# The order of three groups of transfers on SyncE's queue, around a full DMA stretch of a linear-attention and squared-ReLU kernel

## Chip, cores and metric

The kernel runs on one core of a Trainium2 chip. The metric is the device time in microseconds; the median of three runs is given. One further execution was recorded by the profiler.

## The reference

```python
# q, k, v: (8, 8, 576, 64) float32; g_norm: (64,)
kv  = np.einsum('bhsd,bhse->bhde', k, v)
out = np.einsum('bhsd,bhde->bhse', q, kv)
rms = np.sqrt(np.mean(out * out, axis=-1, keepdims=True) + 1e-06)
x   = (out / rms * g_norm)          # then (B,H,S,D) -> (B*S, H*D): 4608 x 512
# w_in: (512, 2048), w_out: (2048, 512), both float64
h = x @ w_in
g = np.maximum(h, 0.0) ** 2
result = g @ w_out                  # 4608 x 512, float32
```

## The kernel before, in words

The work is cut into nine strips of 512 tokens (`for s in range(N_STRIP)`, L1186). Each strip has an up projection with `w_in`, the squared ReLU, and a down projection with `w_out`. Both products are done as seven block products each in place of eight, so the weights are needed as blocks and as sums of blocks. The attention of the coming strips is written in slices between the steps of the projections (`attend`). The order of all instructions is written out by hand: each engine executes its own in the order in which the code issues them. All DMAs that matter here are issued by SyncE (SP) and go into one queue. In the built program each of SP's DMAs also waits, where nothing earlier implies it, for the DMA eight places before it.

The change lies in the first strip (`s == 0`). Its up projection takes 16 steps (`n_up`), its down projection 14 more: seven products in the order 1, 2, 5, 6, 7, 3, 4, two steps each. A step calls `down` (L863), which multiplies (L733), and after a product's second step adds its result into an output or keeps it (`combine`; o_sb at L895 and L897) and may fetch a coming block of `w_out` (`stream`, L828). The sixth product is product 3; its block is the w_blk loaded in the second product's second step, `i == n_up + 3`. The seventh is product 4. PSUM banks are shared: products 1, 6, 7 and 4 use bank A, 5 and 3 bank B, 2 bank C. Product 4 adds into bank A after VectorE has read product 7's result from it.

These parts stand around the change:

- `store_first(b)` (L327, DMA at L329) writes one of three blocks of `w_out`, which the conversion left in unused places of `w_in` in SBUF, to DRAM, in two DMAs of 512 KB. Block 2 is the one moved. These places are needed again: `sums_in` (L295 to L302, subtractions by the helper at L288) writes sums of `w_in` there, so its VectorE instructions wait until the store has read them.
- `load_next(names="kv")` (L131) loads keys and values of one pair of heads, two DMAs of 256 KB. It is called twice, for the third batch's first two pairs.
- `load_rest(2, nc.sync)` (L161) loads keys and values of the third batch's last 64 tokens, two DMAs of 128 KB in rows of 256 B. PE reads both in `key_value` (L431), in the second strip.
- `store_deep_sums` (L849) computes four sums of a `w_out` block on VectorE (tile w_t) and stores them to `w_deep` (L855, L861).

Of the kernel before, what the change touches and what calls it, by code (L numbers as in the profile page):

```python
# [20 lines left out]
def kernel(  # L21
# [135 lines left out]
    def load_rest(b, eng):  # L157
        h = b % 2
        half = slice(REST * h, REST * (h + 1))
        for t, src in ((k_rest[half], k), (v_rest[half], v)):  # L160
            eng.dma_start(out=t, in_=src[b, :, C * P : S].rearrange("h s d -> s h d"))  # L161

    def load_q_rest(b, eng, one=None):
        h = b % 2
        if h == 0 and not one:
            q_rest[b // 2] = rest_pool.tile([P, H, D], FP32, name="q_rest", tag="q_rest")
        src = q[b, :, C * P : S]
        if b < Q_ON_PE:
            eng.dma_start(out=q_rest[b // 2][REST * h : REST * (h + 1)], in_=src.rearrange("h s d -> s h d"))
            return  # L170
        t = squares(q_rest[b // 2])
        for a in range(4) if one is None else (one,):
            hq, f = divmod(a * SQ, D)
            for kq in range(2):
                eng.dma_start(
                    out=t[ts(a, SQ), 2 * h + kq], in_=src[hq::2, ts(kq, SQ), f : f + SQ].rearrange("p i f -> i p f")
                )
# [4 lines left out]
    def load_next(q_eng=nc.sync, names="kvq"):  # L182
        u = next(to_load, None)
        if u is not None:
            load(*u, q_eng, names)
# [6 lines left out]
    def due(queue):  # L192
        if queue and queue[0][0] <= clock[0]:
            _, f, a = queue.popleft()
            f(*a)
            return True
# [4 lines left out]
    def drip(rest=False):  # L201
        for d in (drips, rest_drips) if rest else (drips,):
            if d:
                f, a = d.popleft()
                return f(*a)
# [121 lines left out]
    def store_first(b):  # L327
        for e in range(2):
            nc.sync.dma_start(out=w_out[b, :, e], in_=w_first[b][:, :, ts(e, P)])  # L329

    def convert(n):
        while converted[0] < min(n, len(conversions)):
            fn, a = conversions[converted[0]]
            fn(a)
            converted[0] += 1
# [356 lines left out]
    def attend(n):  # L692
        while slice_at[0] < min(n, len(slices)):
            fn, a = slices[slice_at[0]]
            fn(*a)
            slice_at[0] += 1
# [60 lines left out]
    def sum_g1(s, g):  # L757
        dest = quarters(s, g)
        s1 = gq[s, 1, g] = sum_pool.tile([P, 2, TH], FP32, name="g_s1", tag="sum")
        nc.vector.tensor_tensor(out=s1, in0=dest[12], in1=dest[22], op=ALU.add)  # L760

    def sum_g3(s, g):
        dest = quarters(s, g)
        minus(nc.vector, dest[12], dest[11], dest[12])
# [165 lines left out]
    def leaf_sums(s, p):  # L930
        deque(leaf_steps(s, p), 0)
# [254 lines left out]
    for s in range(N_STRIP):  # L1186
        attend(ready[s])
        if s == DEEP_UP - 1:
            while queried:
                attend(slice_at[0] + 1)  # L1190
            psums.close()
            fpsum = ctx.enter_context(tc.tile_pool(name="fpsum", bufs=5, space=bass.MemoryType.PSUM, reuse_waits="tile"))
            apsum = ctx.enter_context(tc.tile_pool(name="apsum", bufs=1, space=bass.MemoryType.PSUM, reuse_waits="tile"))
        if s >= DEEP_UP:
            steps = [(0.5, up_slot, (s, slot)) for slot in range(55)]
        elif s == 0:
            steps = [(2, up_first, (g, fh, i)) for g in range(NG) for fh in range(2) for i in range(2)]
        else:
            steps = [(1, up, (s, g, p)) for g in range(NG) for p in ORDER]
        n_up = len(steps)  # L1200
        if s < DEEP:

            steps += [(2, down, (s, p, i)) for p in (ORDER if s else (1, 2, 5, 6, 7, 3, 4)) for i in range(2)]
        else:
            steps += [(2, down_deep, (s, k, i)) for k in range(7) for i in range(2)]
        goal, begun = ready.get(s + 1, len(slices)), slice_at[0]
        if s >= DEEP_UP:
            goal = max(goal, min(ready[DEEP_UP] + (len(slices) - ready[DEEP_UP]) * (s - 1) // (N_STRIP - DEEP_UP - 1), len(slices)))
        total, done = sum(w for w, _, _ in steps), 0
        for i, (w, fn, a) in enumerate(steps):  # L1210
            if s == 0 and i < n_up:

                if 4 <= i < 10:
                    convert(3 + i)
                if i == 0:
                    load_next()
                    load_rest(1, nc.sync)
                    load_next()
                if i == 1:
                    load_next()  # L1220
                if i == 2:
                    for b in range(2):
                        load_q_rest(b, nc.sync)
                if i == 14:
                    for b in range(2):
                        store_first(b)
            elif s == 0 and i == n_up:
                convert(len(conversions))
                conv.close()

                stream_pool = ctx.enter_context(tc.tile_pool(name="stream", bufs=4, reuse_waits="tile"))
                sum_pool = ctx.enter_context(tc.tile_pool(name="sum", bufs=8, reuse_waits="tile"))
            if s == 0 and n_up <= i < n_up + 2:
                for g in range(2 * (i - n_up), 2 * (i - n_up) + 2):
                    sum_g1(0, g)
            if s == 0 and n_up + 2 <= i < n_up + 4:
                for g in range(2 * (i - n_up) - 4, 2 * (i - n_up) - 2):
                    sum_g3(0, g)
            fn(*a)
            if s == 0 and i < 4:  # L1240

                convert(3 + i)
            done += w
            if s:
                clock[0] += 3.2 if i >= n_up else 2.2 if s == DEEP else 1.2
                soon = tiles_due and tiles_due[0][2][0] // NT == s + 1
                if i == n_up + 10:
                    while tiles_due and tiles_due[0][2][0] // NT == s + 1:
                        _, f, a = tiles_due.popleft()
                        f(*a)  # L1250
                elif not due(keys_due) and not (soon and due(tiles_due)):
                    least = 2.1 if s == DEEP else 4.5 if i < n_up else 3.3
                    quiet = n_up * 2 // 3 < i < n_up + 3 or s == DEEP and i > n_up + 5
                    if not quiet and clock[0] >= dripped[0] + least:
                        dripped[0] = clock[0]
                        drip(True)
                pace = 25 if s == DEEP else 36
                attend(begun + (goal - begun) * min(i + 1, pace) // pace)
                if s == DEEP and i == n_up - 3:
                    leaf_sums(s, 4)  # L1260
                if s == 1 and i in range(2, 23, 3):
                    deep_sums_in((1, 6, 5, 4, 0, 2, 3)[i // 3])
                if s == 1 and i in (21, 22, 23, 25):
                    stream()
                continue
            if i == n_up:
                stream(2)
            if i == n_up + 3:
                store_first(2)
            if i in (n_up + 8, n_up + 11):  # L1270
                load(2, (i - n_up) // 11, nc.sync, "q")
            if i == n_up + 12:
                load_q_rest(2, nc.sync)
            if i - n_up in (7, 8, 9, 12):
                sums_in((7, 8, 9, 12).index(i - n_up))
            if i == n_up + 11:
                sums_x(1)
            n = i + 1 - (n_up - 6)
            pairs, m = divmod(max(n - 2 * NP, 0), 3)
            attend(min(ready[0] + min(max(n, 0), 2 * NP) + (n >= 2 * NP) + 4 * pairs + (0, 2, 2)[m], goal))  # L1280
            if i == n_up + 6:
                stream()
            while deep_due and i not in (n_up + 1, n_up + 4):
                store_deep_sums(*deep_due.popleft())
            if i == n_up + 2:
                for _ in range(2):
                    load_next(names="kv")
                load_rest(2, nc.sync)
            if 11 <= i < n_up:

                convert((13, 13, 14, 15, 16)[i - 11])
# [30 lines left out]
```

## Time and profile before

| | us |
|---|---|
| median of three runs | 899.84 (899.05 to 900.23) |
| profiled execution, device time | 901.59 |
| span of its instructions | 899.4 |
| TensorE busy | 881.8 |
| VectorE busy | 734.8 |
| ScalarE busy | 315.3 |
| GpSimd busy | 306.6 |
| mean DMA rate over the span | 262 GB/s |
| mean granted TensorE clock | 0.998 |

Times in the profile count from the first instruction of the span. The profiled execution has its own time, 2.2 us more than its span and 1.75 us more than the median of the runs. In the rows, PE is TensorE's matmuls, PEld its weight loads, DVE VectorE, ACT ScalarE, POOL GpSimd and SPq the queue of SyncE, whose rows are DMA issues; "L733" is a line of the kernel; a bracket at the end of a row gives the idle time ahead of it and what ended it. A row of SPq shows how long the issue took. The trace gives the time from issue to landing separately.

### The profile page before, as it was taken

The page shows a single profiled execution, that of the slowest core. Times are in us where ns is not written, and L with a number is a line of the kernel's source. Part 1 is how long each engine was busy: PE and PEld are TensorE (multiplying, and loading weights), DVE is VectorE, ACT ScalarE, POOL GpSimd, SP SyncE. Part 2 cuts the span into 40 slices and gives each one's busy share as a digit, 9 for nine tenths or more (in the row PEclk, how much of TensorE's full clock was granted, in tenths as well). Part 3 has the DMA queues.
Part 4 walks back from the last instruction along what each step waited for, and adds up shares of the span by engine and source line. Part 5 has one row for each costly group of instructions (what it writes and reads, how often), then busy time and mean ns, then how long its engine had stood idle before and what let it go on. Part 6 is the DMA issues. An engine that isn't in the chain of part 4 may idle for free.

```text
span 899.4 us, 20683 instructions
## 1 busy us (share of the span) xinstructions
PE 881.8 (98%) x8296; PEld 824.0 (92%) x8296; DVE 734.8 (82%) x1256; ACT 315.3 (35%) x622; POOL 306.6 (34%) x315
## 2 busy tenths in 40 slices
PE   8999989999999999999999999999999999999998
PEld 7445878889999999999999999999999999999998
DVE  4999979779778986799688966986899779875886
ACT  4898241320026302540245013801271027102710
POOL 0000004900348223731474045704461446144700
PEclk9999999999999999999999999999999999999999
DMA  9998997999988798899886989799647865784385
GB/s 313 298 325 258 291 336 226 279 286 350 304 225 258 272 313 245 192 315 332 241 242 238 320 250 245 228 292 317 209 151 285 296 206 175 285 309 156 124 305 192
DMA packets 169231, 235.71 MB, mean 262 GB/s; under 512 B 79408, under 2 KB 134192, under 8 KB 160688
## 3 DMA queue, kind: packets, MB, share of 16 engines
q1 hardware_dynamic: 168976, 234.40, 81.1%
q8 instruction: 65, 1.06, 0.5%
q14 instruction: 30, 0.25, 0.1%
q10 hardware_dynamic: 160, 0.00, 0.0%
HBM read 197.66 MB, written 36.70 MB: 261 GB/s over the span
## 4 chain that ended last, share of the span: by engine, by line
PE 74%; DVE 10%; DMA 8%; ACT 4%; issue 2%; SPq 1%; DVEq 0%; ACTq 0%
PE ps_B L948 21%; PE ps_A L1136 16%; PE ps_A L948 16%; PE ps_B L1136 8%; PE ps_C L1136 4%; PE ps_A L733 3%; DMA v<-in_v_dram 2%; DMA w_blk<-w_deep 2%; PE kv_ps L431 2%; PE x_ps L467 2%; PE ps_B L733 1%; DVE gt L1148 1%; DMA w_out<-w_in 1%; ACT raw L253 1%; ACT w_c L250 1%
## 5 line engine op out<-in xcount | busy, mean ns | idle before, releaser
L948 PE MATMUL ps_B<-w_blk,g_s 128*128 128x128 f32 x1024 | 126.3, 276 | 0.0
L948 PEld LDWEIGHTS ps_B<-w_blk,g_s 128*128 128x128 f32 x1024 | 120.1, 192 | 0.2
L1136 PE MATMUL ps_A<-x_l,w_in 128*128 128x128 f32 x784 | 104.1, 276 | 0.0
L288 POOL TENSOR_TENSOR x_l<-xT 128x256 f32<-128x256 f32 x21 | 15.8, 751 | 247.7 <-PE ps_A L948 247.7
L948 PE MATMUL ps_B<-w_blk,gt 128*128 128x128 f32 x768 | 97.5, 276 | 0.9 <-DMA w_blk<-w_deep 0.9
L1136 PEld LDWEIGHTS ps_A<-x_l,w_in 128*128 128x128 f32 x784 | 95.4, 192 | 0.5 <-DVE gt L1148 0.2
L948 PE MATMUL ps_A<-w_blk,g_s 128*128 128x128 f32 x768 | 93.6, 276 | 0.0
L948 PEld LDWEIGHTS ps_B<-w_blk,gt 128*128 128x128 f32 x768 | 91.6, 192 | 1.1 <-DMA w_blk<-w_deep 1.1
L948 PEld LDWEIGHTS ps_A<-w_blk,g_s 128*128 128x128 f32 x768 | 89.7, 192 | 0.0
L1148 POOL TENSOR_TENSOR snap<-snap,gt 128x512 f32<-128x512 f32 x35 | 46.6, 1330 | 119.3 <-ACT snap L1153 55.0
L1153 ACT COPY snap<-ps_A 128x512 f32<-128x512 f32 x63 | 36.6, 581 | 133.5 <-PE ps_A L1136 117.7
L1086 ACT ACTIVATE gt<-gt 128x512 f32<-128x512 f32 x112 | 69.6, 622 | 18.1 <-DVE gt L1148 18.0
L963 DVE TENSOR_TENSOR o_sb<-o_sb,ps_B 128x256 f32<-128x256 f32 (+1 forms) x128 | 49.5, 387 | 31.5 <-ACT o_sb L964 24.1
L948 PE MATMUL ps_A<-w_blk,gt 128*128 128x128 f32 x576 | 72.4, 276 | 0.3 <-DMA w_blk<-w_deep 0.3
L1087 ACT ACTIVATE gt<-gt 128x512 f32<-128x512 f32 x112 | 70.6, 631 | 3.6
L948 PEld LDWEIGHTS ps_A<-w_blk,gt 128*128 128x128 f32 x576 | 68.2, 192 | 0.7 <-DMA w_blk<-w_deep 0.5
L1148 POOL TENSOR_TENSOR gt<-gt,snap 128x512 f32<-128x512 f32 x42 | 52.5, 1277 | 23.5 <-DVE snap L1148 23.5
L1046 POOL TENSOR_TENSOR w_i<-w_in 128x512 f32<-128x512 f32 x7 | 10.6, 1513 | 145.7 <-DMA q<-in_q_dram 145.0
L288 DVE TENSOR_TENSOR gt<-gt 128x2048 f32<-128x2048 f32 (+1 forms) x29 | 59.7, 2064 | 0.1
L964 ACT COPY o_sb<-ps_A 128x128 f32<-128x128 f32 x24 | 6.4, 265 | 146.6 <-PE ps_A L948 146.6
L1136 PE MATMUL ps_A<-x_l,w_blk 128*128 128x128 f32 x392 | 52.2, 277 | 1.3 <-issue 1.2
L1136 PE MATMUL ps_B<-x_l,w_blk 128*128 128x128 f32 x392 | 52.0, 276 | 0.0
(180 smaller groups left out, 1814.5 us busy)
## 6 DMA issues: line engine op xcount, KB each, us to landing
w_blk<-w_deep SPq DMA_DIRECT2D x56, 1024.0 KB, 6.8
w_blk<-w_out SPq DMA_DIRECT2D x56, 768.0 KB, 6.1
w_blk<-w_in_deep SPq DMA_DIRECT2D x49, 768.0 KB, 5.4
raw<-in_moe_w_in_dram SPq DMA_DIRECT2D x16, 512.0 KB, 7.6
raw<-in_moe_w_out_dram SPq DMA_DIRECT2D x16, 512.0 KB, 5.9
k<-in_k_dram SPq DMA_DIRECT2D x29, 256.0 KB, 5.0
v<-in_v_dram SPq DMA_DIRECT2D x29, 256.0 KB, 5.5
x_d<-x_q SPq DMA_DIRECT2D x27, 256.0 KB, 4.9
```

The lines of the kernel that those rows point to most:

```text
L288: eng.tensor_tensor(out=out, in0=a, in1=b, op=ALU.subtract)
L431: nc.tensor.matmul(ps[ts(h, D), i], lhsT=a, rhs=w, start=i == 0 and c == 0, stop=c == C, skip_group_check=True)
L467: nc.tensor.matmul(ps[half, r, i, ts(p, D)], lhsT=q[row, half], rhs=kvd[b, p][row, row], start=True, stop=True)
L733: nc.tensor.matmul(bank[BANK[p]][:, i, :], lhsT=lhsT(k), rhs=rhs(k), start=p in (1, 5, 2) and i == 0 and k == 0, stop=k == n - 1, skip_gro ...
L948: nc.tensor.matmul(chain[c][x][:, i, :], lhsT=a[:, f, :], rhs=w[:, f, :], start=x not in opened[c] and f == 0, stop=f == FQ // 2 - 1, skip ...
L963: add = lambda out, a, b: nc.vector.tensor_tensor(out=out, in0=a, in1=b, op=ALU.add)
L1046: nc.gpsimd.tensor_tensor(out=s1, in0=w_half(b, 0, 1), in1=w_half(b, 1, 1), op=ALU.add)
L1086: nc.scalar.activation(o, o, AF.Relu)
L1087: nc.scalar.activation(o, o, AF.Square)
L1136: nc.tensor.matmul(ps[:, i, :], lhsT=w, rhs=rhs, start=j in (1, 2, 5) and i == 0, stop=True, skip_group_check=True)
L1148: add = lambda eng, out, a, b: eng.tensor_tensor(out=out, in0=a, in1=b, op=ALU.add)
L1153: nc.scalar.copy(t, ps)
```

## The change

The two DMAs of `store_first(2)` are issued one step earlier, ahead of the two pairs' k and v loads. `load_rest(2, nc.sync)` is issued one step later, behind the load of product 3's block and the first output store, both issued inside that step by `down`. No other instruction changes, and the engines other than SP keep their order.

```diff
             if i == n_up:
                 stream(2)
-            if i == n_up + 3:
-                store_first(2)
             ...
             while deep_due and i not in (n_up + 1, n_up + 4):
                 store_deep_sums(*deep_due.popleft())
             if i == n_up + 2:
+                store_first(2)
                 for _ in range(2):
                     load_next(names="kv")
+            if i == n_up + 3:
                 load_rest(2, nc.sync)
```

SP's order in this stretch, with the size of each DMA:

```
before: 2 x w_deep (1 MB) | k, v, k, v (256 KB) | k_rest, v_rest (128 KB) | block of product 3 (1 MB) | output (256 KB)
        | 2 x store_first(2) (512 KB) | w_deep (1 MB) | block of product 4 (1 MB)
after:  2 x w_deep (1 MB) | 2 x store_first(2) (512 KB) | k, v, k, v (256 KB) | block of product 3 (1 MB) | output (256 KB)
        | k_rest, v_rest (128 KB) | w_deep (1 MB) | block of product 4 (1 MB)
```

## The prediction

> **What bounds the kernel now.** I read the page's busy table first, then the list of waits, then the stretch around the moved instructions in the timelines of PE, DVE and SP.
>
> ```profile
> PE 881.8 (98%) x8296; PEld 824.0 (92%) x8296; DVE 734.8 (82%) x1256; ACT 315.3 (35%) x622; POOL 306.6 (34%) x315
> ```
>
> TensorE is busy for 98% of the span, so only what shortens or fills its gaps can move the end. The list of waits names who ended each gap of PE:
>
> ```profile
> PE ps_A L733 <- DVE o_sb L897: 3.8, 1, 3.8
> ...
> PE ps_B L948 <- DMA w_blk<-w_deep: 0.9, 1, 0.9
> ...
> PE kv_ps L431 <- DMA v<-in_v_dram: 0.4, 1, 0.4
> ```
>
> The columns are total us, times, longest. The largest single gap of the kernel is one of 3.8 us, and it lies just behind the change. PE's timeline shows it:
>
> ```profile
> 125.34 7.07 PE L733 MATMUL ps_B<-w_blk,gt 128*128 128x256 f32 x32
> 136.18 8.77 PE L733 MATMUL ps_A<-w_blk,gt 128*128 128x256 f32 x32 [3.77 <-DVE o_sb L897]
> ```
>
> The first row is product 3 of the first strip's down projection (the sixth in its order), the second is product 4 (the seventh). Product 4 adds into the bank that product 7 used, so it needs VectorE to have read that bank (o_sb, L897). VectorE is late:
>
> ```profile
> 124.76 0.69 DVE L288 TENSOR_TENSOR w_in<-w_in 128x512 f32<-128x512 f32 x1
> 129.04 1.30 DVE L288 TENSOR_TENSOR w_in<-w_in 128x512 f32<-128x512 f32 x2 [3.58 <-DMA w_out<-w_in]
> ...
> 135.44 0.68 DVE L897 TENSOR_TENSOR o_sb<-ps_A,snap 128x512 f32<-128x512 f32 x1
> ```
>
> It stood 3.58 us until the store of W_out's third first block had read the place that `sums_in` overwrites, and from 129.04 to the o_sb it has no gap. The store was issued late:
>
> ```profile
> 108.18 0.56 SPq L131 DMA_DIRECT2D k<-in_k_dram  x1
> ...
> 114.97 1.82 SPq L828 DMA_DIRECT2D w_blk<-w_out  x1
> 116.89 0.61 SPq L847 DMA_DIRECT2D out_dram<-o_sb  x1
> 117.55 4.66 SPq L329 DMA_DIRECT2D w_out<-w_in  x2
> ...
> 125.85 0.37 SPq L828 DMA_DIRECT2D w_blk<-w_out  x1
> ```
>
> And the DMA engines are full here. The busy times by stretch:
>
> ```profile
> 102.00:136.00 34.00, 30.41 (x207) 26.35 (x205) 28.80 (x48) 12.09 (x13) 0.00 (x0) 1.00 1.00 324
> 136.00:152.00 16.00, 15.82 (x122) 13.26 (x122) 15.76 (x22) 2.35 (x4) 4.61 (x3) 0.89 0.68 209
> ```
>
> The last three columns are the granted clock, the DMA share and GB/s. From 102 to 136 the DMA share is 1.00. Also, the second stretch has a clock of 0.89: half clock for 3.41 us from 136.02, just after the gap.
>
> **What the Trainium skill says.** "DMA: Bandwidth & Descriptors", section "Queues, rings and completion order": on each DMA engine descriptors are consumed in ring order, though completions need not follow it. The trace agrees on the order here: every transfer issued from 102 to 126 landed in the order of issue, each 9 to 11 us after it once the queue was full. The same page, "Anatomy of one DMA": waits are taken on the issuing sequencer, not by the DMA engines. So a moved DMA delays all behind it on SP, and nothing ahead of it. "TensorE: Matmul & The Clock Gate", section "What's actually happening": an idle window of 3413 ns puts the array at half clock, and the windows run free of the kernel. The trace agrees: a gap of 3.77 us, then 3.41 us at half clock, in which matmuls start 0.427 us apart in place of 0.216.
>
> **The change part by part.** Nothing is added or removed; PE, DVE, ACT and POOL keep their order. On SP two stores (2 x 512 KB) go from behind product 3's block and the output store to ahead of the k and v loads, and two rest loads (2 x 128 KB, rows of 256 B) go from ahead of that block to behind the output store.
>
> *The store.* It is issued behind the w_deep stores, near 108.2 instead of 117.55. Those land at 116.75. The stores cost 1.51 and 1.66 us of the full queue (before: landings 125.75 of the output store, then 127.26 and 128.92). So they land near 116.75 + 3.17 = 119.9. VectorE asks at 125.45 (124.76 + 0.69). The 3.58 us wait goes, and all of VectorE's work behind it moves up by as much: o_sb ends at 136.12 - 3.58 = 132.5.
>
> *The k and v loads* (4 x 256 KB) land 3.17 us later, the last at 120.48 + 3.17 = 123.7. PE reads them at 150.87: free. *The rest loads* landed at 121.60 and 122.43; now they land behind the output store, near 129. PE reads them at 151.96: free. If the cover failed, PE would wait for them us by us.
>
> *Product 3's block* (1 MB) landed at 125.06. Ahead of it come the stores, 3.17 us more, and the rest loads leave, which took 121.60 - 120.48 = 1.12 and 0.83 us, 1.95 less. It lands at 126.3 if it keeps its own 2.63 us. The like block before it took 4.84 us behind its neighbour (106.91 to 111.75), and product 4's took 4.55 (131.22 to 135.77): with those it lands at 128.2 to 128.5. I take 127, bounds 126 and 129.5. Product 3 then starts at 127 instead of 125.34 and ends near 134.1 (7.07 us). This costs nothing as long as product 4 is held by something later; that is the next step.
>
> *Product 4's block* (1 MB) is what is late next. It landed at 135.77, 0.35 us ahead of VectorE's o_sb: two waits that were nearly equal. The same bytes stand ahead of it in both orders (stores, k, v, rest, block 3, output, w_deep), and the queue never runs dry, so I keep 135.8, bounds 135.0 and 136.6 for a changed mix of reads and writes. Product 4 starts at 135.85 instead of 136.18. Of the 3.77 us that VectorE's wait cost, **0.33 us** come back; the rest is a DMA wait that was hidden behind it. The gap splits in two, about 1.6 us ahead of product 3 and 1.7 ahead of product 4.
>
> *The clock.* Two gaps of less than 3.41 us can't hold an idle window. In the profiled execution the half clock costs product 4 8.77 - 7.10 = **1.67 us**, and this should be absent. But the windows run free: a gap of 3.77 us holds a whole one in (3.77 - 3.41)/3.41, a tenth of all phases, if the window must be wholly idle. The profiled execution took 901.59 against a median of 899.84, 1.75 more, which fits runs that mostly lack the half clock. So against the median I take nothing (bounds 0 and 1.67).
>
> *Behind it.* VectorE has no gap from 129.04 to the last w_t at 152.7, whose w_deep store held SP until 152.75, ahead of the next k and v loads. All this comes up to 3.6 us earlier, while PE comes 0.3 us earlier. PE's wait of 0.40 us for v at 166.23 goes: **0.4 us**. The wait of 0.87 us for a w_deep block at 231.3 has its issue set by buffers that PE frees, in a stretch with DMA 97% busy; some of its neighbours come earlier. I take half, **0.4 us**, bounds -0.5 and 0.87.
>
> *Sum:* 0.33 + 0.4 + 0.4 = 1.13, rounded to 1.2 us. Against the profiled execution (901.59, of which the span is 899.4) it is 1.2 + 1.67 = 2.9 us: near 898.7. Against the median, 899.84 - 1.2 = **898.6 us**, 0.13%. A measurement of this kernel can tell about 0.2%, 1.8 us, from no change.
>
> **The rivals.**
>
> *The half clock is in most runs before, or product 4's block lands earlier.* For it: the one execution with a trace has the half clock. Against: its time stands 1.75 above the median. With the clock in, 898.6 - 1.67 = 896.9. If block 4 were also in place when VectorE is done (132.5), the whole gap would go: 899.84 - 3.77 - 0.8 = 895.3 without the clock. Speaking against that: 34 us of full DMA with the same bytes. Chance of faster by over 0.2%: 0.33.
>
> *Slower: product 3's block becomes the bound.* The idle time ahead of product 3 begins at 125.5. If the block lands after 128.9, the gap exceeds 3.41 us and can bring the half clock to product 3; at 129.5 product 3 ends at 129.5 + 7.07 + 1.67 = 138.2, and product 4 starts 2.0 us later than before: 901.8, less what comes back behind it. Even without the half clock, the block decides from a landing of 136.18 - 7.07 = 129.1 on. For it: blocks of this kind took 4.55 to 4.84 us when not behind the small rest rows. Against: even with those it lands at 128.5. Chance of slower by over 0.2%: 0.12.
>
> *No change in the time:* one wait takes the place of the other, as worked out. Between 898.0 and 901.6, likeliest 898.0 to 900.2: 0.55. The issue does move, so "it doesn't do what it says" isn't open.
>
> **How the numbers follow.** The point is that of the exchange of waits, 898.6. Downward the range takes in the half clock (896.9) and a little of an earlier block, 896.6; upward the late block 3, partly paid back, 901.0. Outside lie the rest of the slower case and the full gain, together under 2 in 10.
>
> **What would show it.** Right: in the changed trace VectorE's wait for w_out is gone; the stores land by 121; PE waits 1 to 3 us ahead of product 3 and for w_blk ahead of product 4, which starts between 135.0 and 136.6; the clock stays at 1.00 there; the wait for v near 166 is gone. Wrong: product 4 starting by 134 (the queue wasn't the bound), product 3 starting after 129, or a new DMA wait between 150 and 240 that eats the gain.

## The result, and the profile after

In 20 runs of each, the changed kernel took 897.61 us (median; 894.86 to 902.88) against 899.93 us before: a ratio of 0.9975, 95% interval 0.9962 to 0.9988, from which one run of before that took 1117.07 us is left out. Two later sets of the same kernel gave 0.9986 (0.9978 to 0.9995) and 0.9981 (0.9972 to 0.9991). So the gain is near 0.2%, 1.8 us: just about what a measurement of this kernel can tell.

The profiled execution of after took 894.9 us, the second shortest of its 20 runs. Its span is 892.9 us against 899.4, and this difference of 6.5 us must not be taken for the gain. Here is its row of busy times, then what its list of waits says of PE (total us, times, longest):

```profile
PE 879.6 (99%) x8296; PEld 822.6 (92%) x8296; DVE 733.9 (82%) x1256; ACT 315.6 (35%) x622; POOL 306.7 (34%) x315
```

```profile
PE ps_A L733 <- DVE gt L796: 0.9, 1, 0.9
...
PE ps_A L733 <- DVE o_sb L897: 0.4, 1, 0.4
...
PE ps_B L948 <- DMA w_blk<-w_deep: 0.2, 1, 0.2
```

The wait of 3.8 us for o_sb is down to 0.4, the wait for v is gone, and a wait of 0.9 us for VectorE that before did not have has come (`gt`, L796, in the second strip's up projection). PE's timeline and VectorE's:

```profile
124.29 7.14 PE L733 MATMUL ps_B<-w_blk,gt 128*128 128x256 f32 x32
131.79 7.17 PE L733 MATMUL ps_A<-w_blk,gt 128*128 128x256 f32 x32 [0.36 <-DVE o_sb L897]
```

```profile
123.30 2.02 DVE L288 TENSOR_TENSOR w_in<-w_in 128x512 f32<-128x512 f32 x3
...
128.52 0.69 DVE L288 TENSOR_TENSOR w_t<-w_blk 128x512 f32<-128x512 f32 x1 [0.54 <-DMA w_deep<-w_t]
...
131.06 0.68 DVE L897 TENSOR_TENSOR o_sb<-ps_A,snap 128x512 f32<-128x512 f32 x1
```

Product 3 starts without a gap, product 4 follows after 0.36 us and takes 7.17 us in place of 8.77. VectorE no longer waits for w_out in `sums_in`; it waits 0.54 us for another transfer, the w_deep store whose buffer it fills again. The DMA issues in SP's order, and the busy times of two stretches (clock, DMA share, GB/s last):

```profile
107.63 3.65 SPq L329 DMA_DIRECT2D w_out<-w_in  x2
111.32 3.56 SPq L131 DMA_DIRECT2D k<-in_k_dram  x1
...
116.85 0.41 SPq L828 DMA_DIRECT2D w_blk<-w_out  x1
117.35 0.38 SPq L847 DMA_DIRECT2D out_dram<-o_sb  x1
117.79 1.83 SPq L161 DMA_DIRECT2D k_rest<-in_k_dram  x1
...
121.81 0.36 SPq L828 DMA_DIRECT2D w_blk<-w_out  x1
```

```profile
101.00:131.00 30.00, 30.00 (x205) 26.11 (x205) 28.62 (x47) 12.09 (x13) 0.00 (x0) 1.00 0.99 349
131.00:147.00 16.00, 15.64 (x134) 12.99 (x133) 15.76 (x23) 2.86 (x6) 3.99 (x3) 1.00 0.77 241
```

The stores move up as the diff says. The DMA engines are as busy as before (0.99), but move 349 GB/s where they moved 324. The k, v and rest loads, which now land later (the last k or v at 121.63, the last rest load at 126.04), cost PE no wait.

### The profile page after: what moved, and what is told of

Its sections match the earlier page's. It is cut to its first block, busy times and chain, and to the rows that moved or that the text cites. A ratio compares the mean times of both kernels' runs of the same rounds, so it can differ in the third digit from the quotient of the medians.

```text
span 892.9 us, 20684 instructions
## 1 busy us (share of the span) xinstructions
PE 879.6 (99%) x8296; PEld 822.6 (92%) x8296; DVE 733.9 (82%) x1256; ACT 315.6 (35%) x622; POOL 306.7 (34%) x315
## 4 chain that ended last, share of the span: by engine, by line
PE 74%; DVE 15%; DMA 6%; issue 3%; ACT 2%; SPq 1%; DVEq 0%; POOL 0%; ACTq 0%; POOLq 0%
PE ps_B L948 22%; PE ps_A L948 17%; PE ps_A L1136 16%; PE ps_B L1136 8%; PE ps_C L1136 4%; DVE w_t L288 2%; PE kv_ps L431 2%; PE x_ps L467 1%; DVE w_c L268 1%; PE ps_A L733 1%; DVE gt L1148 1%; DVE wt L288 1%; DMA w_deep<-w_t 1%; DMA w_blk<-w_deep 1%; DMA raw<-in_moe_w_out_dram 1%
## 5 line engine op out<-in xcount | busy, mean ns | idle before, releaser
L948 PE MATMUL ps_B<-w_blk,g_s 128*128 128x128 f32 x1024 | 126.2, 275 | 0.0
L948 PEld LDWEIGHTS ps_B<-w_blk,g_s 128*128 128x128 f32 x1024 | 120.0, 192 | 0.2
L1136 PE MATMUL ps_A<-x_l,w_in 128*128 128x128 f32 x784 | 104.1, 276 | 0.0
L948 PE MATMUL ps_B<-w_blk,gt 128*128 128x128 f32 x768 | 97.6, 275 | 0.2 <-DMA w_blk<-w_deep 0.2
L1136 PEld LDWEIGHTS ps_A<-x_l,w_in 128*128 128x128 f32 x784 | 95.4, 192 | 0.5 <-DVE gt L1148 0.2
L948 PE MATMUL ps_A<-w_blk,g_s 128*128 128x128 f32 x768 | 93.6, 275 | 0.0
L948 PEld LDWEIGHTS ps_B<-w_blk,gt 128*128 128x128 f32 x768 | 91.5, 192 | 0.5 <-DMA w_blk<-w_deep 0.4
L948 PEld LDWEIGHTS ps_A<-w_blk,g_s 128*128 128x128 f32 x768 | 89.6, 192 | 0.0
L948 PE MATMUL ps_A<-w_blk,gt 128*128 128x128 f32 x576 | 72.2, 275 | 0.0
L948 PEld LDWEIGHTS ps_A<-w_blk,gt 128*128 128x128 f32 x576 | 68.2, 192 | 0.0
L1136 PE MATMUL ps_A<-x_l,w_blk 128*128 128x128 f32 x392 | 52.2, 276 | 1.3 <-issue 1.2
L1136 PE MATMUL ps_B<-x_l,w_blk 128*128 128x128 f32 x392 | 52.0, 276 | 0.0
```

The costliest lines, as they stand in the source:

```text
L948: nc.tensor.matmul(chain[c][x][:, i, :], lhsT=a[:, f, :], rhs=w[:, f, :], start=x not in opened[c] and f == 0, stop=f == FQ // 2 - 1, skip ...
L1136: nc.tensor.matmul(ps[:, i, :], lhsT=w, rhs=rhs, start=j in (1, 2, 5) and i == 0, stop=True, skip_group_check=True)
```

## The experiments

To compare traces, the span is cut at four events of PE: the start of product 6 (the first row `ps_A<-w_blk`), the end of product 4, the first matmul of the second strip's down projection (L948), and the first of the third strip's up projection (L1136); the last piece ends with PE's last product. Products go by their numbers (in the order 1, 2, 5, 6, 7, 3, 4). The table has the length of each piece in us, from PE's timeline, with the landings of blocks 3 and 4 counted from the start of product 6. PE asks for block 3 at 14.9, when product 7 is done. "Drain" is the time from the landing of product 6's block to that of block 4; where a number stands, the same transfers of 8.5 MiB land in it.

| trace | block 3 | block 4 | drain | product 6 to end of 4 | to L948 | to L1136 | to the end |
|---|---|---|---|---|---|---|---|
| before | 14.58 | 25.29 | 28.86 | 34.46 | 57.65 | 42.22 | 650.5 |
| before, again | 14.39 | 24.64 | 28.14 | 34.18 | 57.63 | 41.09 | 649.6 |
| after | 14.79 | 21.45 | 25.09 | 29.61 | 58.47 | 41.70 | 649.7 |
| after, again | 18.07 | 24.31 | 27.59 | 33.95 | 57.01 | 41.09 | 649.7 |
| after, third | 15.19 | 21.67 | 25.66 | 29.78 | 59.23 | 42.01 | 650.8 |
| store alone | 19.68 | 25.31 | 28.49 | 35.46 | 57.20 | 41.09 | 649.6 |
| rest alone | 11.65 | 22.00 | 25.36 | 29.76 | 59.52 | 41.39 | 649.6 |
| rest alone, again | 12.42 | 23.57 | 26.50 | 30.84 | 58.63 | 43.10 | 649.6 |
| rest later | 12.05 | 22.33 | - | 29.95 | 57.49 | 42.48 | 649.6 |
| k, v, rest late | 11.69 | 20.71 | - | 30.32 | 59.53 | 41.94 | 649.6 |
| k, v behind 3 | 12.85 | 23.99 | 28.23 | 31.27 | 58.40 | 41.09 | 650.4 |
| whole, rest later | 17.01 | 22.55 | - | 31.20 | 57.97 | 41.93 | 653.7 |
| identity products in the gap | 14.14 | 24.91 | 28.81 | 32.36 | 60.00 | 43.02 | 650.2 |
| sums later | 14.63 | 25.04 | 28.54 | 32.31 | 63.78 | 41.09 | 649.7 |

The theory to begin with was the forecast's own (A): block 4's landing is set by the bytes ahead of it. Its rival (B): the new order makes the queue drain faster.

**Both kernels again.** No edit.

> The kernel before, unchanged, for a second trace and the granted clock of each run. In the one trace of the changed kernel the block of product 4 landed 4 us earlier than forecast. Theory A (the forecast: the landing is set by the bytes ahead, and that trace was a fortunate one): the landing varies from run to run by a few us in both kernels, so in this second trace of before it may lie anywhere from 131 to 137 us; ratio 1.000. Theory B (the new order itself lets the queue drain faster): here the block lands at 135 to 136.5 again, product 4 starts near 136, VectorE waits 3 to 4 us for w_out. Both: ratio 1.000 within 0.2%. The half clock after the gap, if its windows run free, should be missing in most runs; a run that has it shows a clock of 0.998, one without it 1.000.

> The changed kernel, unchanged, for a second trace. Theory A: the block of product 4 lands anywhere from 131 to 137 us, and product 4 starts with it or with VectorE's o_sb near 132.5, whichever is later. Theory B: it lands at 130 to 132 again, product 4 starts before 133 and is held by VectorE. Both: faster than before by 0.1 to 0.4%.

Before against itself: 1.0007 (0.9998 to 1.0016). After against before: 0.9986 (0.9978 to 0.9995). In the second trace of before VectorE waited 3.51 us and product 4 followed a gap of 3.39 us, as in the first; block 4 landed 24.64 us after the start of product 6, near the 25.29 of the first. The half clock, expected to be missing in most runs, was there in 12 of 13 by their granted clock (0.998 or less). The second trace of after looks quite different from its first, in PE's timeline:

```profile
127.87 8.83 PE L733 MATMUL ps_B<-w_blk,gt 128*128 128x256 f32 x32 [3.19 <-DMA w_blk<-w_out]
136.54 7.07 PE L733 MATMUL ps_A<-w_blk,gt 128*128 128x256 f32 x32
```

Here the gap is ahead of product 3, which waits 3.19 us for its block and then runs 1.7 us longer at half clock. Block 4 had landed at 133.97, but PE was still at product 3: neither theory had that. The piece up to the end of product 4 took 33.95 us, hardly less than before. So after has two courses: block 3 lands in time, or some 3 us late.

**A third trace of after.** No edit.

> The changed kernel again, for a third trace beside the parts below on the same chip. If block 3's landing decides: a gap ahead of product 3 of between 0 and 3.5 us, with the landing, and if it exceeds about 3 us a half clock behind it; most runs without half clock; faster than before by 0.12 to 0.3%.

0.9981 (0.9972 to 0.9991), as expected. Block 3 came 0.3 us late:

```profile
126.16 7.14 PE L733 MATMUL ps_B<-w_blk,gt 128*128 128x256 f32 x32 [0.30 <-DMA w_blk<-w_out]
133.44 7.17 PE L733 MATMUL ps_A<-w_blk,gt 128*128 128x256 f32 x32
```

Three traces, with block 3 at 14.79, 15.19 and 18.07 against the 14.9 at which PE asks: the change puts this block right at its limit.

**The store alone.** The rest loads keep their place.

```diff
-            if i == n_up + 3:
-                store_first(2)
...
             if i == n_up + 2:
+                store_first(2)
                 for _ in range(2):
                     load_next(names="kv")
                 load_rest(2, nc.sync)
```

> One part alone: the store of W_out's third first block ahead of the k and v loads, the rest loads left ahead of product 3's block. VectorE's wait for w_out goes as in the whole change. Product 3's block has the stores (3.2 us) ahead of it and keeps the rest loads: by the forecast's sums it lands at 125.1 + 3.2 = 128.2 in place of 125.1, product 3 ends at 135.3, product 4 starts near 136. Theory A: no gain but for the half clock, 0 to 0.1% faster than before. Theory B (early stores let the queue drain faster): product 3's block lands before 127, product 4 starts before 134, faster by 0.15 to 0.3%.

0.9997 (0.9988 to 1.0005): no gain that can be told, as A has it, though block 3 landed 2 us later than in A's sums (19.7 against 17.7 us after the start of product 6). It comes 4.8 us late and the half clock follows:

```profile
129.04 8.73 PE L733 MATMUL ps_B<-w_blk,gt 128*128 128x256 f32 x32 [4.80 <-DMA w_blk<-w_out]
```

VectorE's wait for w_out is gone here too. Taking away the wait that the profile of before showed, by itself, brings nothing.

**The rest loads alone.** The store keeps its place.

```diff
                     load_next(names="kv")
-                load_rest(2, nc.sync)
+            if i == n_up + 3:
+                load_rest(2, nc.sync)
```

> The other part alone: the rest loads go behind product 3's block, the output store and the two stores; the stores keep their place behind the output store. The stores land some 2 us earlier than before (near 127), so VectorE's wait falls from 3.6 to about 1.6 us and its o_sb ends near 134.1. Theory A: block 4 lands at 135 to 136, product 4 starts with it, 0 to 0.1% faster. Theory B, if the rest loads' place makes the queue drain faster: block 4 lands by 134 and product 4 starts at 134.1 with VectorE, 0.15 to 0.25% faster; if the stores' place makes it, as in theory A.

> The rest loads moved alone, again (7 timed runs of it came through so far). If moving the rest loads is the part that pays: faster than before by 0.2 to 0.35% and faster than the whole change of this same set; block 3 lands near 122, no gap ahead of product 3, gap of under 1.5 us ahead of product 4, clock 0.999 or more in nearly all runs. If the first result was luck: within the whole change's interval, 0.1 to 0.25%.

0.9973 (0.9963 to 0.9984) and, in the second set, 0.9977 (0.9966 to 0.9988): at least the gain of the whole change, which had 0.9986 and 0.9981 in these two sets; the intervals overlap. PE's and VectorE's rows of the first trace:

```profile
125.14 7.07 PE L733 MATMUL ps_B<-w_blk,gt 128*128 128x256 f32 x32
132.86 7.17 PE L733 MATMUL ps_A<-w_blk,gt 128*128 128x256 f32 x32 [0.65 <-DVE o_sb L897]
```

```profile
125.72 1.29 DVE L288 TENSOR_TENSOR w_in<-w_in 128x512 f32<-128x512 f32 x2 [0.46 <-DMA w_out<-w_in]
```

The store keeps its place behind the output; with the rest loads gone from ahead of it, it was issued 2.4 us earlier (115.16 against 117.55) and its second half landed 3.3 us earlier (125.60 against 128.92), where 2 us were expected. So VectorE's wait fell from 3.5 to 0.46 us. The whole drain was shorter too: 25.4 and 26.5 us in place of 28.1 to 28.9. A's premise falls: the same transfers do not take the same time. In the second trace product 4 waited 1.77 us for its block, more than the 1.5 us expected, and the gain is not told apart from that of the whole change in its set.

**k and v further back.** First all six loads behind block 4, the store left in place; then, with the whole change, k and v behind block 3 and the output.

```diff
# k, v, rest late (from before)
-            if i == n_up + 2:
-                for _ in range(2):
-                    load_next(names="kv")
-                load_rest(2, nc.sync)
...
             if i == n_up + 6:
                 stream()
+                for _ in range(2):
+                    load_next(names="kv")
+                load_rest(2, nc.sync)
# k, v behind 3 (from after)
             if i == n_up + 2:
                 store_first(2)
+            if i == n_up + 3:
                 for _ in range(2):
                     load_next(names="kv")
-            if i == n_up + 3:
                 load_rest(2, nc.sync)
```

> The four k and v loads and both rest loads go behind the block of product 4; the stores stay behind the output store. 1.28 MB leave from ahead of both blocks and of the stores. Theory C (the order of bytes on the full queue decides when blocks 3 and 4 and the stores land, and this decides the gap): block 3 lands by 121, the stores by 124, block 4 by 131; no gap over 0.7 us between products 7 and 4, no half clock, 0.25 to 0.4% faster than before, with little spread between runs. Theory D (the gain comes from the second strip: k, v and q loads further back): k, v and rest now land latest, near 135 to 140, PE's waits near 145 to 170 grow, no gain over the whole change.

> As the whole change, but the four k and v loads go behind product 3's block and the output store too, ahead of the rest loads. Ahead of block 3 there are now the stores (3.2 us) in place of k, v and rest (3.7 + 2.0 us). Theory C: block 3 lands at 121 to 125 in each run, before PE asks for it, and the stores near 118 to 120; block 4 has the same bytes ahead as before and lands at 131 to 135; at most one gap of 0 to 3 us ahead of product 4, 0.2 to 0.35% faster than before. Theory D: as the whole change, 0.15 to 0.25%.

0.9973 (0.9963 to 0.9982) and 0.9978 (0.9967 to 0.999). With the loads late, block 3 lands 3 us before PE asks for it and no half clock follows in 13 of 14 runs, but the gap ahead of product 4 was 1.2 us and not under 0.7: VectorE, which had waited only 0.35 us for w_out, was busy up to then. And 1.07 us go to a wait for v near 163. So C is right on the direction (block 3 landed at 121.72, the stores at 125.92, block 4 at 130.74, the first two later than it said), and D on a part of the time: the second strip asks for something back. In the other kernel block 3 is in time and block 4 is the one that PE waits for, 2.2 us, with a drain of 28.23 us, as slow as before although the rest loads are behind block 3; the clock was 0.998 or less in 6 of its 9 runs.

**The rest loads later still**, behind block 4; then the same line in the changed kernel, with the store ahead of k and v.

```diff
-                load_rest(2, nc.sync)
+            if i == n_up + 6:
+                load_rest(2, nc.sync)
```

> As the rest loads moved alone, but behind the block of product 4 and the four w_deep stores. Theory C: block 3 and the stores land as in that kernel (122 and 125.6), block 4 some 0.8 to 1.9 us earlier than there (132.3), near 131; product 4's gap of 0.65 us was VectorE's, so it stays: within 0.1% of that kernel, 0.2 to 0.35% faster than before. PE needs the rest loads near 146 and they land by 136: free. Theory D (the rest loads' narrow rows slow what runs beside them, wherever they stand): the w_deep stores or the q loads beside them land 1 us later, still no effect on PE.

> The whole change with the rest loads still further back, behind the block of product 4 and the four w_deep stores. It differs from the kernel that has only the rest loads there (0.9963 of before) by the store ahead of the k and v loads. If block 3's landing decides, the early store costs here: block 3 lands 3 us later than there, at 124 to 127, a gap of 0 to 3 us opens ahead of product 3, half clock in some runs, 0.1 to 0.3% faster than before, that is slower than with the store left behind. If VectorE's wait for the store decides, it is at least as fast, 0.37% or more.

0.9963 (0.9953 to 0.9973), and with the store ahead 0.9958 (0.9943 to 0.9973). The two lowest ratios, though their intervals touch those of other kernels in their sets (the changed kernel, run beside the second, had 0.9981, 0.9972 to 0.9991); between the two nothing can be told. In the trace with the store ahead block 3 is 2.13 us late again, and its piece is longer than with the store behind (31.20 against 29.95 us), as expected. But its runs are not slower, which was expected only if VectorE's wait decides. That execution took 900.13 us, the longest of its 8, with a half clock at 565 us that no other trace has, so what the early store is worth once the rest loads are away stays open.

**The half clock by itself.** 14 products of the identity with itself between products 3 and 4; their result is not read.

```diff
+            if s == 0 and i == n_up + 12:
+                keep_busy(apsum.tile([P, C, P], FP32, name="t_ps", tag="at")[:, 0], 14)
```

> The kernel before, with 14 products of the identity matrix with itself (their results are never read) put on PE between products 3 and 4. They should take 14 x 0.22 = 3.1 us, inside the gap of 3.4 to 3.8 us in which PE waits for product 7's bank. Nothing else moves. Theory: the half clock costs about 1.6 us in most runs of before (a clock of 0.998 or less in 82 of 95 of them) and comes from the idle gap; so here the clock is 0.999 or more in most runs, product 4 takes 7.1 us in place of 8.8, and the kernel is faster by 0.12 to 0.2% although the wait is as long as before. Rival: the half clock is no cost on the path (what comes behind waits for other engines anyway): within 0.05%.

1.0012 (1.0001 to 1.0023): not faster, if anything slower. The half clock was gone from 13 of 14 runs, and product 4 took 7.17 us (the profile counts two matmuls for each of the 14 products):

```profile
132.36 3.29 PE L375 MATMUL t_ps<-ident 128*128 128x128 f32 x28
135.78 7.17 PE L733 MATMUL ps_A<-w_blk,gt 128*128 128x256 f32 x32
```

What PE waited for in the 100 us behind it:

```profile
PE ps_B L948 <- DMA w_blk<-w_deep: 1.2, 2, 0.7
PE ps_A L733 <- DVE gt L796: 0.9, 1, 0.9
PE ps_B L948 <- DMA w_blk<-w_out: 0.7, 1, 0.7
PE x_ps L467 <- DVE qT L383: 0.6, 1, 0.6
PE xt_ps L595 <- DVE x_n L535: 0.3, 1, 0.3
```

These are 3.7 us, against 1.3 (0.40 and 0.87) in the same part of before's trace. The first piece is 2 us shorter, the next two 2.4 and 1.4 us longer. VectorE, whose work was not moved, is the one that PE then waits for, and behind it the blocks. So the theory fails, and the rival is right in its reason: what was won locally was waited for later. That the half clock costs nothing is not shown by this kernel alone, since it also adds work to PE. Why it came out slower and not equal was not settled.

**VectorE's order.** SP as before; `sums_in(0)` to `(2)` come two steps later, behind product 7's o_sb.

```diff
-            if i - n_up in (7, 8, 9, 12):
-                sums_in((7, 8, 9, 12).index(i - n_up))
+            if i - n_up in (9, 10, 11, 12):
+                sums_in((9, 10, 11, 12).index(i - n_up))
```

> SP's order is that of before, but sums_in(0), (1) and (2) are called two steps later, so that VectorE reads product 7's bank (o_sb) ahead of its wait for w_out, not behind it. This asks whether the block of product 4 stood hidden behind VectorE's wait, as forecast. Theory C (it did): o_sb ends near 128 to 130, product 4 is now released by its block's landing, 133.9 to 135.8 in the two traces of before, and starts 0.4 to 0.6 us earlier than there; the gap is still 2.5 to 3.3 us, so the half clock stays in most runs; 0 to 0.1% faster. Theory D (the block was not close behind): product 4 starts before 132, no half clock, 0.3 to 0.5% faster.

1.0045 (1.0031 to 1.0059), slower, against both theories. On the question asked, C is right: product 4 is now released by its block, which landed at 134.60, after a gap of 3.2 us. But o_sb did not come early, since behind the wait for w_out stood another:

```profile
130.44 0.69 DVE L288 TENSOR_TENSOR w_t<-w_blk 128x512 f32<-128x512 f32 x1 [7.53 <-DMA w_deep<-w_t]
```

The sums for product 7 go into the buffer from which product 5's sums are being stored, and that store lands near 130. And the sums of `w_in` came late for the second strip:

```profile
PE ps_A L733 <- DVE gt L796: 4.3, 1, 4.3
PE ps_A L733 <- DMA w_blk<-w_out: 3.2, 1, 3.2
PE ps_A L733 <- DVE o_sb L897: 0.4, 1, 0.4
```

## Why the prediction was right, and where it was not

The forecast was 898.6 us, 0.13% faster; measured were 0.25, 0.14 and 0.19%. The time lies inside the range, but the way to it does not hold. Its own sign of being wrong, product 4 starting by 134 us, was there in two of the three traces (131.79 and 133.44). Of its steps:

- *The store and VectorE's wait.* Right. The stores landed at 116.38 and 117.98 (forecast near 119.9 on before's clock, of which after's is 1.1 us ahead at the start of product 6), the wait for w_out is gone in all three traces. Not foreseen: the next wait on VectorE, for the w_deep store of product 5's sums, of 0.5, 0.9 and 2.7 us.
- *Block 3.* The forecast was too late for two of the three traces. It had 127 (bounds 126 and 129.5) on before's clock, that is 16.5 after the start of product 6 (15.5 to 19.0); the traces had 14.8, 15.2 and 18.1. So PE's forecast wait of 1 to 3 us ahead of product 3 was 0, 0.3 and 3.19 us. The rival that ends slower, in which block 3 becomes the bound and brings the half clock, is what one trace in three shows; there it took nearly all the gain of its piece away (33.95 us against 34.2 to 34.5) but made nothing slower.
- *Block 4 lands as before, since the same bytes stand ahead of it.* This step failed. Forecast 25.3 after the start of product 6, bounds 24.5 to 26.1; measured 21.5, 21.7 and 24.3. The waits were nearly equal in before, as said (the experiment with VectorE's order shows it), but they did not exchange: where block 3 came in time, both went. The drain took 25.1 to 27.6 us and not 28.1 to 28.9. It took 28.1 to 28.9 in all five traces with the rest loads ahead of block 3, and 25.1 to 27.6 in five of six with them behind it. So their place matters, but it is not all: one trace (28.23) doesn't follow. Two parts can be read from the traces. The two rest loads took 1.4 to 2.0 us of the queue, from landing to landing, ahead of block 3, and 0.8 to 1.3 us behind it. And a slow drain moved more: 9.5 to 9.7 MB in the seven of 27.6 us and more, 9.1 to 9.2 MB in the three of 25.7 us and less, where the 8.5 MiB that had to land are 8.9 MB. So in a slow drain more of the transfers behind block 4 was moved before the last part of block 4 had landed. Equal bytes ahead of a transfer do not fix its landing; what holds its last part back is not shown.
- *The clock.* The step "a tenth of all phases" failed: 112 of 133 timed runs of before had a clock of 0.998 or less, and 11 of 61 of after. So the 1.75 us by which the profiled execution stood above the median were no sign that most runs lack the half clock. And a gap of less than 3.41 us can bring it (3.19 us in the second trace of after); the last section shows why. But the value taken for it, nothing, came out right for another reason: taking it away alone brought no gain, and in the three later sets before's 100 runs with it have a median of 899.58 us, the 20 without it 899.92.
- *Behind it.* The forecast had 0.8 us more gain there. The sign was wrong where block 3 came in time: of 4.7 and 4.5 us won up to the end of product 4 (against the mean of before's two traces, 34.32), the second strip's up projection gave back 0.8 and 1.6 us (58.47 and 59.23 against 57.64), with new waits for VectorE in it, and its down projection up to 0.4 (42.01 against 41.65). Left are 3.8 and 2.6 us in such runs; in the second trace, 0.4 + 0.6 + 0.6 = 1.6 us over the three pieces. The gain measured, 1.3 to 2.3 us in the three sets, lies at the low end of that. How often each course occurs can only be guessed from the clock: of after's timed runs the 11 with 0.998 or less had a median of 899.48 us, the 50 others 897.63.

So it was luck that the sum came out near the truth: two of its terms were wrong in opposite directions, a much larger local gain than forecast where block 3 came in time, and a loss behind it in place of a gain.

Which part of the change pays is settled: the rest loads. The store, which ended the wait in the profile of before, gives nothing alone.

## What to carry to other kernels

When the wait that a profile names is on a full DMA queue, ask what lands last among all transfers of that stretch: moving a transfer up moves others down, and the named wait can go without any gain. In this kernel it paid to put transfers that are needed 20 us later behind those needed now, and the two rest loads gave as much as all six loads together (0.9973 each). That their narrow rows are the reason was not tested. And one profiled execution is one draw: here three traces of the same program differ by 4 us at one place, more than the whole change is worth.

## What the runs showed of the hardware

- The half clock begins on a fixed grid: in the first trace of before it came at 136.02 and again, after the last instruction, at 900.61, which is 224.0 windows of 3413 ns later; in the second trace of after 225.0 windows lie between 128.32 and 896.32. That agrees with the free-running window of 3413 ns that the Trainium skill gives ("TensorE: Matmul & The Clock Gate", "What's actually happening"). But the window need not be wholly idle, which the forecast had assumed. With the grid laid over all 14 traces, the half clock followed each window in which PE was busy for about 1.54 us or less, and none in which it was busy for 1.55 us or more (the ends of matmuls are modelled, so this limit is rough). So a gap of 1.87 us that lay within one window brought it, and a gap of 3.24 us that a boundary divided did not. The rows give start and end, length and PE's busy time, and, third from the end, the clock:

```profile
561.83:565.24 3.41, 1.54 (x14) 1.35 (x12) 3.41 (x7) 2.21 (x5) 3.25 (x5) 1.00 0.99 263
565.25:568.66 3.41, 3.41 (x17) 3.17 (x17) 1.97 (x4) 2.61 (x5) 0.74 (x2) 0.50 0.86 245
```

```profile
129.74:133.15 3.41, 1.76 (x9) 1.20 (x7) 2.67 (x5) 0.00 (x0) 0.00 (x0) 1.00 0.97 320
133.15:136.57 3.42, 1.84 (x9) 1.66 (x10) 3.35 (x6) 0.00 (x0) 0.00 (x0) 1.00 0.95 267
136.57:139.98 3.41, 3.41 (x17) 3.01 (x16) 3.31 (x6) 0.00 (x0) 0.00 (x0) 1.00 0.81 318
```

  The first pair is from the trace with the rest loads later and the store ahead, the other rows are from the one with VectorE's order changed. An estimate from these numbers: a gap escapes the half clock only if a boundary cuts it into two parts that are both under 1.87 us (3.41 less 1.54). For before's gaps of 3.4 to 3.8 us that is at most a tenth of all phases, (3.74 - 3.39)/3.41: the reverse of the forecast's tenth, and near the 112 of 133 runs that had it.
- The same transfers of 8.5 MiB went through a queue that was never empty in 25.1 to 28.9 us, depending on the order and, within one order, on the run (25.1 and 27.6 us for the changed kernel). A transfer's landing is not the moment at which the DMA engines go on to the next one: in the slowest drains some 0.8 MB of what was issued behind block 4 had been moved before block 4 landed.
